# Sparse attention and a mixture of attention experts on one core: a new order of loads and TensorE steps, epsilons as columns of the sums, k's low half on GpSimd

## The chip, the core and the metric

The kernel runs on one core of a Trainium2 chip. A core has a matrix engine (TensorE, PE in the profile; its weight loads are shown apart as PEld), a vector engine (VectorE, DVE), a scalar engine (ScalarE, ACT), GpSimd (POOL) and SyncE (SP), which issues the DMA transfers of this kernel. Each engine works through its own list of instructions in order; semaphores let it wait for others. TensorE writes to the eight banks of PSUM; VectorE and ScalarE copy from there to SBUF. The metric is the device time of one execution in microseconds, lower is better.

## What is computed

The reference has two parts. The first is attention over q, k, v of shape (8, 8, 576, 64), batch, heads, tokens, width. Heads 0 to 3 have a local causal mask (the last 32 tokens), heads 4 to 7 a strided one (earlier tokens of the same place modulo 32). Both are normalised with exp and a sum to which 1e-9 is added. The eight heads side by side are x, 576 tokens by 512.

```python
mask_local   = (rel >= 0) & (rel < stride)
mask_strided = (rel >= 0) & (pos[None, :] % stride == pos[:, None] % stride)
attn = np.exp(scores - max); attn /= attn.sum(-1) + 1e-09; x = attn @ v
```

The second part is a mixture of four experts, each a causal attention head over x with its own wq, wk, wv, wo. A gate picks two of the four experts for each token and weighs them with a softmax (again with 1e-9 in the sum).

```python
logits = x @ w_gate; topk = two largest; w = softmax(topk logits, + 1e-09)
for e: q, k, v = x @ wq[e], x @ wk[e], x @ wv[e]
       ye = causal_softmax(scale * q @ k.T, + 1e-09) @ v @ wo[e]
       out += (w of e, 0 if not picked) * ye
```

## The kernel before

A batch goes through two stages. **Stage 1** (`stage1`, L422) does the sparse attention of two heads at a time, four pairs of heads a batch. q and k are loaded and turned (L493), the scores of the few blocks that the mask leaves are computed by small matmuls (step `s_l` for a local pair, L534, 36 products; `s_s` for a strided one, L541, 22), masked (L557), and put through a softmax of six steps (L563 to L579): maximum, subtraction on GpSimd, exp, sum, epsilon and reciprocal (L576, L577), product on GpSimd. Then the values: `xa_l` (L629, 42 products) for a local pair; `pt` (L600) and `xa_s` (L652) for a strided one. The result is split in a high and a low part, xh and xl (L612, L614), since later matmuls work on pairs of a high and a low half.

**Stage 2** (L695 to L982) projects x: `pj` (L777; L788 in the first batch) for q and k of two experts at a time, `vp` (L706) for v and the gate. Of k three things are kept: the high half, a plain copy kf (L800), and the low half kf minus high (L806), which VectorE or GpSimd computes as the order says. The gate follows (L734 to L765). Then, for each tile of 128 tokens, the scores `s2` (L876; `s2_4`, L833, for the last 64 tokens), mask and maximum (L883), exp with its sum (L888), epsilon and reciprocal of the sums (`recip2`, L894 and L895), scaling by it and by the gate's weight on GpSimd (`scale2`, L915 and L906), transposing (`t2`, L934), copying out (L303), and the product with v (`acc`, L967). `out_tile` (L984) multiplies by wo (`yp`, L996), and SyncE stores the result (L1008).

The operations are recorded first (`op`, L91), each with its kind, its engines and what it reads and writes. The order in which they are put out is a table written by hand or by a planner: the string PLAN (L115), a word for each operation. `schedule` (L272) reads it:

```python
for word in PLAN.split():
    o, slots = OPS[int(word[:i])], iter(word[i + 1:])
    for u in o.uses:
        if not u.taken: u.ring.take(u, int(next(slots)))
    o.fn(ENGINE[word[i]])
```

The number is the operation, the letter the engine (P, A, D, G, S), the digits behind it the buffers that the operation takes. So the table sets the order on each engine, SyncE's queue among them, and the choice between two engines where an operation allows it. Products of plain fp32 appear in the trace as two matmuls with two weight loads each (72 for an `s_l` step, 84 for an `xa_l` step, 44 for `xa_s`), those of the split halves as one. `spin` (L1012) are matmuls of a constant tile fz that compute nothing; they stand where the table puts them, 54 of the 60.

Of the kernel before, what the change touches and what calls it, by code (L numbers as in the profile page):

```python
# [20 lines left out]
def attention_moe_kernel(  # L21
# [69 lines left out]
    def op(kind, eng, n, key, fn, r=(), w=(), mode=None, npk=0, after=()):  # L91
# [29 lines left out]
        114D 251S0 17P5 115D 48P2 23P1 116D1 47P6 146P0 152S 117D 118G 110S 119G 120A 185P31 147D 121A 122D 191P7
        153S 186A 123D 252A0 124D 156P520 192A 253G0 233S 40P4 268S4 157D 125G 46P1 302S 158D 41P6 35P0 126G 273S
        159D2 33P3 28P7 160D 154S 189P4 161G 127D1 267S 162G 163A 187P5 190D 234A 164A 235G 165D 128P162000 155S
        188A 166D 167D 271S 89P374511 169G 131A 150S 135A 132D 129A 136D 133A 168G 130D 39P6 134D 96A 92A 199P011
        137G 97D 90A 93D 94A 98G 245S 91D 95D 170P261 195S0 200D 18P5 201D 172A 1246P70 171A 202D3 9P3 203D 1296P41
        204G 239S 275D0 1289P0 248S 205G 206A 49P5 173P6122 246A 208D 207A 247G 196S 1253P2 209D 174A 178A 1260P3
        175D 193S 176A 1297P 179D 177D 1247P 240A 197S 210D 180G 1254P 241G 1248P 249A 194S 211G 1266P5 250D 31P1
        198S 212G 42P6 1267P 303S 1261P 1290P 254S1 213P160 1268P 215A 214D 300S 25P6 0P1 216P6133 337S0 257S 1298P
        221A 217A 1291P 222D 219A 255A 1262P 220D 338S1 218D 256G 1303P1 260S0 1299P 308D1 223G 266S 1255P 1301A0
        306S2 1249P 1300A 1304P 304S 1302D0 1250A 1263P 258A 263S1 1251A1 1269P 259D 269S 1264A 1252G1 1292P 1271A  # L130
        1270A 1265D 305S 1305P 1294A 1272D 474S3 1281P61 1293A 261A0 336S 1295D 341S 1275P4 262D0 1282A 334S 346S1
        264A 1318P730 274D 1276A 265G 335S 1323P500 307S 1320D0 280P640 1324D 1322A 411S4 1325D 1326A 1256P 1319D
        281D 1327A 1309P3 282D 1257A 340S 1277P5 1258A 283D0 339S 1321A 1259G 342D0 284G 1310P 1278A 1306P 309D
        375S0 1279P0 1307A 347S 285A 1308D 374S 286D 1273P7 1280A 377S 343D 407S2 348S 1283P6 1328P420 1274A 287D
        1284A 344S 288G 1285D00000 1311P 370S1 1312P 413S 45P5 1313A 312S2 1329D 1286A 1314A 1317P1001 1330D 1331A
        1287D 5P7 1332A 1349P650 1315D 349S 1288G 1333D 1385P421 1351D1 1337G 372S 1316P73 406S 1350D 1336G 1353A
        373S 1335G 1354D 350P560 1352A 371S 1338G 1386D2 279S0 1355D 1388A 1334G 352D 1339G 1340P742 1356A 351D 376S
# [150 lines left out]
    def ring(tag, shape, bufs, dtype=F32):  # L288
        return Ring(tag, shape, dtype, bufs, pool=sb)

    def fixed(tag, shape, bufs, dtype=F32, value=None):
        ts = []
        for i in range(bufs):
            t = const.tile(shape, dtype, name=f"{tag}{i}")
            if value is not None:
                for x in value(t):
                    nc.vector.memset(x, 0.0)
            ts.append(t)
        return Ring(tag, shape, dtype, bufs, tiles=ts)
# [775 lines left out]
```

## Time and profile before

| | |
|---|---|
| time, median of 3 runs | 470.14 us (468.7 to 471.44) |
| the profiled execution: its time | 472.47 us |
| its span, first to last instruction | 470.3 us |
| mean granted clock of TensorE | 0.979 |
| busy share: TensorE, VectorE, ScalarE, GpSimd | 94%, 77%, 58%, 44% |
| DMA packets, bytes | 189816, 41.90 MB |

The busy share of an engine is the time covered by its instructions. A wait is idle time just before an instruction, with the engine and line that ended it; "issue" stands where nothing that the profile shows was waited for. [...]

### The profile page before, as it was taken

To read this page: it belongs to the slowest core of one execution; us is meant where nothing else is said; L and a number is where in the kernel's file an instruction comes from. 1 tells how busy PE (TensorE), PEld (TensorE's weight loads), DVE (VectorE), ACT (ScalarE), POOL (GpSimd) and SP (SyncE) were. 2 spreads that over 40 slices of the span, in tenths; PEclk is the share of its full clock that TensorE was granted. 3 is DMA by queue.
4 is the path that set the end of the run, shared out by engine and by line. 5 is a ranking of instruction groups with operands and counts; after the bars stand their busy time and mean duration, and the time that the engine had idled before them with its cause. 6 is when DMAs were issued, how large, how long until landed. Compare 5 with 4: busy or idle time off the path is not lost.

```text
span 470.3 us, 19348 instructions
## 1 busy us (share of the span) xinstructions
PE 441.2 (94%) x7876; PEld 389.9 (83%) x7876; DVE 360.6 (77%) x1078; ACT 272.9 (58%) x835; POOL 208.3 (44%) x324
## 2 busy tenths in 40 slices
PE   7999997879997999989899989999999899999996
PEld 7898975759976998889789968799879898899874
DVE  4566699956898997798699969888999679735740
ACT  2444648725667565866377554844785367745752
POOL 6354237733067643552274505571557207700540
PEclk9989998889999999999999999999999989999999
DMA  6654855543664535441564642456542310110113
GB/s 180 140 102 83 149 94 94 93 81 52 122 141 93 94 71 110 100 102 32 103 108 89 134 85 50 92 94 124 106 111 60 93 48 2 57 46 0 48 68 112
DMA packets 189816, 41.90 MB, mean 89 GB/s; under 512 B 184064, under 2 KB 184064, under 8 KB 189728
## 3 DMA queue, kind: packets, MB, share of 16 engines
q1 hardware_dynamic: 189728, 40.67, 41.6%
q8 instruction: 62, 1.02, 0.9%
q14 instruction: 26, 0.21, 0.2%
HBM read 31.20 MB, written 9.44 MB: 86 GB/s over the span
## 4 chain that ended last, share of the span: by engine, by line
PE 77%; DVE 12%; issue 4%; POOL 2%; DMA 1%; ACT 1%; SPq 1%; DVEq 0%; ACTq 0%; POOLq 0%
PE bank L777 18%; PE bank L996 9%; PE bank L706 9%; PE bank L967 8%; PE bank L876 6%; PE bank L934 5%; PE bank L629 3%; PE bank L652 3%; PE bank L534 3%; PE bank L788 3%; DVE p L883 2%; PE bank L461 2%; PE bank L1015 2%; PE bank L541 2%; PE bank L714 2%
## 5 line engine op out<-in xcount | busy, mean ns | idle before, releaser
L915 POOL TENSOR_SCALAR p<-p,st,wt 128x256 f32<-128x256 f32 (+3 forms) x128 | 77.1, 614 | 74.7 <-PE bank L777 23.3
L888 ACT ACTIVATE p<-p,st 128x128 f32<-128x128 f32 (+3 forms) x128 | 71.7, 563 | 12.7 <-DVE st L883 12.6
L883 DVE CUSTOM_DVE_ANT_0 p<-bank,m_cau 128x512 f32<-128x512 f32 (+3 forms) x128 | 57.1, 483 | 2.9 <-PE bank L876 2.1
L493 DVE STREAM_TRANSPOSE qkt<-nat 128x576 f32<-128x576 f32 x56 | 56.0, 1008 | 2.9 <-DMA nat<-in_q_dram 1.9
L303 ACT COPY th<-bank 128x256 f32<-128x256 f32 (+2 forms) x112 | 43.7, 429 | 12.7 <-PE bank L934 9.6
L967 PE MATMUL bank<-th,vs 128*64 128x192 f32 (+4 forms) x512 | 49.1, 343 | 0.0
L967 PEld LDWEIGHTS bank<-th,vs 128*64 128x64 f32 x512 | 34.8, 139 | 14.3 <-issue 6.9
L934 PE MATMUL bank<-ident,p 64*128 64x64 f32 x800 | 41.4, 234 | 3.6 <-POOL p L915 1.6
L934 PEld LDWEIGHTS bank<-ident,p 64*128 64x128 f32 x800 | 34.9, 144 | 11.7 <-issue 3.7
L797 ACT CAST qk<-bank 128x288 fp32r<-128x288 f32 x64 | 25.6, 402 | 28.0 <-PE bank L777 25.8
L614 DVE TENSOR_TENSOR xl<-bank,xh 128x160 fp32r<-128x160 f32 (+3 forms) x112 | 30.5, 323 | 14.5 <-ACT xh L612 13.0
L706 PE MATMUL bank<-wh_v,xh 128*128 128x260 f32 x128 | 36.8, 287 | 0.0
L706 PE MATMUL bank<-wl_v,xh 128*128 128x260 f32 x128 | 36.3, 283 | 0.0
L706 PE MATMUL bank<-wh_v,xl 128*128 128x260 f32 x128 | 36.0, 281 | 0.0
L612 ACT CAST xh<-bank 128x128 fp32r<-128x128 f32 (+3 forms) x112 | 27.4, 327 | 14.5 <-PE bank L629 7.3
L777 PE MATMUL bank<-xh,wh_k 128*128 128x288 f32 x112 | 33.8, 302 | 0.0
L777 PE MATMUL bank<-xh,wh_q 128*128 128x288 f32 x112 | 33.5, 299 | 0.2 <-DVE p1s L557 0.2
L777 PE MATMUL bank<-xl,wh_k 128*128 128x288 f32 x112 | 33.0, 294 | 0.0
L777 PE MATMUL bank<-xh,wl_k 128*128 128x288 f32 x112 | 33.0, 294 | 0.0
L777 PE MATMUL bank<-xl,wh_q 128*128 128x288 f32 x112 | 33.0, 294 | 0.0
L777 PE MATMUL bank<-xh,wl_q 128*128 128x288 f32 x112 | 33.0, 294 | 0.0
L420 POOL CAST xh<-xl 128x64 fp32r<-128x64 f32 x32 | 7.5, 237 | 56.2 <-DVE xl L614 56.1
(161 smaller groups left out, 1278.7 us busy)
## 6 DMA issues: line engine op xcount, KB each, us to landing
out_dram<-ys SPq DMA_DIRECT2D x32, 256.0 KB
nat<-in_q_dram SPq DMA_DIRECT2D x112, 72.0 KB
nat<-in_k_dram SPq DMA_DIRECT2D x112, 72.0 KB
v<-in_v_dram SPq DMA_DIRECT2D x96, 40.0 KB
v<-in_v_dram SPq DMA_DIRECT2D x128, 22.5 KB
v<-in_v_dram SPq DMA_DIRECT2D x64, 27.0 KB
v<-in_v_dram SPq DMA_DIRECT2D x32, 48.0 KB
out_dram<-ys SPq DMA_DIRECT2D x8, 128.0 KB
```

The source lines that it names most:

```text
L303: (nc.scalar.copy if e == "ACT" else nc.vector.tensor_copy)(dst, src)
L493: nc.vector.transpose(dst, src)
L614: op("xl", "D", n_, key + 0.5, lambda e, s_=s_, x_=x_: nc.vector.tensor_sub(x_(xl.t), s_(xa.t), x_(f(xh.t))), r=[xa, xh[u]], w=[xl[u]])
L706: nc.tensor.matmul(vp.t[:m, :NV], xx.t[:, t0:t0 + m], ww.t[:, kt, :], start=i == 0, stop=i == 11)
L777: nc.tensor.matmul(pj.t[:, :HS], ww.t[:, kt, ep * 128:(ep + 1) * 128], xx.t[:, c], start=i == 0, stop=i == 11)
L876: nc.tensor.matmul(sp[a].t[:, :nk], x.t[r, 0, q0:q0 + 128], y.t[r, 1, :nk], start=i == 0, stop=i == 2)
L883: lambda e, sp=sp, p=p, a=a, nk=nk, ci=ci: nc.vector.tensor_tensor_reduce(out=p.t[:, a, :nk], in0=sp[a].t[:, :nk], in1=m_cau[:, S - nk:], ...
L888: op("exp2", "A", nk, k_ + 1, lambda e, p=p, a=a, ci=ci, nk=nk: nc.scalar.activation(p.t[:, a, :nk], p.t[:, a, :nk], AF.Exp, bias=st.t[:, ...
L915: lambda e, p=p, a=a, ci=ci, t=t, nk=nk: nc.gpsimd.tensor_scalar(p.t[:, a, :nk], p.t[:, a, :nk], st.t[:, 14 + ci + a:15 + ci + a], wt.t[:, ...
L934: nc.tensor.transpose(tp[hf].t[:, 64 * c:64 * c + 64], src, ident[r, r])
L967: nc.tensor.matmul(acc.t[o, c0:c0 + cn], vw, th[a].t[:, s0:s0 + cn], start=j == 0, stop=j == idx[-1], skip_group_check=True)
L996: nc.tensor.matmul(yp.t[:, :DM], xx.t[:, c0:c0 + 128], ww.t[:, ep, :], start=i == 0, stop=i == 5)
```

## The change

The table PLAN is new from end to end. Of its first lines:

```diff
-        99S0 4P0 100S1 10P1 139S0 34P2 109S0 1P3 11P4 61S2 44P5 301S3 30P6 236S0 38P7 71S1 7P0 37P1 230S1 21P2 6P3
...
+        242S0 43P0 230S1 17P1 60S0 44P2 151S0 29P3 7P4 99S1 38P5 61S2 28P6 243A0 110S1 12P7 231A0 21P0 236S2 232G0
...
```

Three places show what it does. On TensorE, in the part of the program where the second batch's stage 1 ends and the third one's begins, the order before runs from the end of an `xa_l` step (L629) through a whole `xa_s` step into two `s_l` steps (L534, for the buffers qkt_183 and then qkt_181) and on to `pt` (L600):

```order
L629 MATMUL bank_68<-pt_197,v_189 64x32 x2
L652 MATMUL bank_64<-pt_198,v_187 64x54
...
L652 MATMUL bank_64<-pt_198,v_187 64x36 x2
L534 MATMUL bank_65<-qkt_183 32x64
...
L534 MATMUL bank_67<-qkt_183 32x64
L534 MATMUL bank_68<-qkt_181 32x64
...
L534 MATMUL bank_66<-qkt_181 32x64
L600 MATMUL bank_69<-ident,p1s_194 128x64
```

At the same place the new order has one `s_l` step (now L535) between `xa_l` (L634) and an output step `yp` (L1003), then transposing (L941), and `pt` (L605):

```order
L634 MATMUL bank_70<-pt_198,v_187 64x32 x2
L535 MATMUL bank_67<-qkt_183 32x64
...
L535 MATMUL bank_69<-qkt_183 32x64
L1003 MATMUL bank_71<-wh_o_258,oh_238 128x512
...
L1003 MATMUL bank_71<-wl_o_259,oh_239 128x512
L941 MATMUL bank_66<-ident,p_169 128x64
...
L941 MATMUL bank_70<-ident,p_169 128x64
L605 MATMUL bank_68<-ident,p1s_194 128x64
```

The second `s_l` step of the pair stands later, behind `yp`, two `xa_s` and an `acc` step.

The second place is the beginning of SyncE's queue (nat, vs and p hold q and k of the first batch, v its values, th weights). Before:

```order
L445 DMA nat_176<-in_q_dram 128x576
L445 DMA nat_177<-in_k_dram 128x576
L450 DMA vs_174<-in_q_dram 36x1024
L504 DMA v_185<-in_v_dram 32x5x64 x2
L445 DMA nat_178<-in_k_dram 128x576
```

Now:

```order
L388 DMA th_170<-in_moe_wq_dram 128x4x64
L388 DMA th_171<-in_moe_wk_dram 128x4x64
L446 DMA nat_176<-in_q_dram 128x576
L512 DMA v_185<-in_v_dram 18x6x64 x2
L446 DMA nat_177<-in_q_dram 128x576
L446 DMA nat_178<-in_k_dram 128x576
```

Two loads of weights and one of q stand ahead of the first load of v, where three of q and k stood.

The third place is GpSimd's list, in the second batch of stage 2. In the new order the gate's product (L765) is followed by six scalings (L922) and then by a low half of k (L812), which only GpSimd computes now:

```order
L765 TENSOR_TENSOR wt_225<-sel_221,mx_223 128x20
L765 TENSOR_TENSOR wt_225<-sel_221,mx_223 64x2 x2
L922 TENSOR_SCALAR p_165<-p_165,st_234,wt_225 128x384
L922 TENSOR_SCALAR p_162<-p_162,st_234,wt_225 128x256
L922 TENSOR_SCALAR p_160<-p_160,st_234,wt_225 128x128
L922 TENSOR_SCALAR p_165<-p_165,st_234,wt_225 128x384
L922 TENSOR_SCALAR p_162<-p_162,st_234,wt_225 128x256
L922 TENSOR_SCALAR p_160<-p_160,st_234,wt_225 128x128
L812 TENSOR_TENSOR qkl_156<-kf_159,qk_155 128x288
```

Before, 13 of the 32 low halves of k stood on GpSimd and 19 on VectorE.

The other edits follow. A column that holds 1e-9 for good stands beside the sums, so that one reduction over the sums and that column, or over a pair of columns, adds it; the separate additions go. In stage 1 the strided tile has room for the column beside its 54 scores, the local one adds a pair. The gate's last product moves from VectorE to GpSimd.

```diff
-    fz = const.tile([128, 128], F32, name="fz")
+    fz = const.tile([128, 1], F32, name="fz")
...
-    PSR = fixed("p1s", [128, 2, 6, 64], 2, value=lambda t: [t[:, h, :, 54:] for h in range(2)])
+    PSR = fixed("p1s", [128, 2, 6, 64], 2, value=lambda t: [(t[:, h, :, 54:], EPS) for h in range(2)])
-    ST1 = ring("st1", [128, 3, 12], 4)
+    ST1 = fixed("st1", [128, 4, 12], 4, value=lambda t: [(t[:, 3, :], EPS)])
...
             elif step == 3:
+                P = P if local else p.t[:, hsl, :, :nk + 1]
                 nc.vector.tensor_reduce(R[1], P, axis=mybir.AxisListType.X, op=ALU.add)
             elif step == 4:
-                nc.vector.tensor_scalar_add(R[2], R[1], EPS)
-                nc.vector.reciprocal(R[2], R[2])
+                if local:
+                    s = st.t.rearrange("p j i -> p (j i)")
+                    nc.vector.tensor_reduce(s[:, 24:24 + 2 * ni], at(s, 0, 128, 12, [[1, 2 * ni], [24, 2]]),
+                                            axis=mybir.AxisListType.X, op=ALU.add)
+                nc.vector.reciprocal(R[2], R[2 if local else 1])
...
-    LSEL = ring("sel", [128, NT, E], 1)
+    LSEL = fixed("sel", [128, NT, E + 1], 1, value=lambda t: [(t[:, :, E:], EPS)])
-    ST2 = ring("st2", [128, 24], 6)
+    ST2 = fixed("st2", [128, 30], 6, value=lambda t: [(t[:, 24:], EPS)])
...
-        def gate2(e):
-            w_ = wt.t[:, :NT]
-            nc.vector.tensor_mul(w_, w_, sel.t)
-            nc.vector.tensor_reduce(mx.t, w_, axis=mybir.AxisListType.X, op=ALU.add)
-            nc.vector.tensor_scalar_add(mx.t, mx.t, EPS)
+        def gate3(e):
+            s_ = sel.t[:, :, :E]
+            nc.vector.tensor_mul(s_, s_, wt.t[:, :NT])
+            nc.vector.tensor_reduce(mx.t, sel.t, axis=mybir.AxisListType.X, op=ALU.add)
             nc.vector.reciprocal(mx.t, mx.t)
-            nc.vector.tensor_mul(w_, w_, mx.t.unsqueeze(2).to_broadcast([128, NT, E]))
+
+        def gate4(e):
+            for r, t0, o, c in ((slice(0, 128), slice(0, NT), wt.t[:, :NT], slice(0, E)),
+                                (slice(0, 64), NT - 1, wt.t[0:64, NT, 0:2], slice(0, E, 3)),
+                                (slice(64, 128), NT - 1, wt.t[64:128, NT, 0:2], slice(1, 3))):
...
+                nc.gpsimd.tensor_tensor(o, sel.t[r, t0, c], m_, ALU.mult)
...
-                op("pj_lo", "DG", HS, key + step * u + 0.8, lambda e, c_=c_: (nc.gpsimd if e == "POOL" else nc.vector).tensor_sub(
+                op("pj_lo", "G", HS, key + step * u + 0.8, lambda e, c_=c_: nc.gpsimd.tensor_sub(
...
-            nc.vector.tensor_scalar_add(st.t[:, 14:14 + ncol], st.t[:, 8:8 + ncol], EPS)
+            nc.vector.tensor_reduce(st.t[:, 14:14 + ncol], at(st.t, 0, 128, 8, [[1, ncol], [16, 2]]),
+                                    axis=mybir.AxisListType.X, op=ALU.add)
...
-           lambda e: nc.tensor.matmul(wb.t[:, :128], fz, fz, start=True, stop=True), w=[wb], mode=M128)
+           lambda e: nc.tensor.matmul(wb.t[:, :128], fz.to_broadcast([128, 128]), fz.to_broadcast([128, 128]), start=True, stop=True), w=[wb], mode=M128)
```

The table holds 55 of the `spin` matmuls now. All other TensorE steps are the same in kind and number.

## Rows read from the trace of the kernel before

**Rows 1.** Page, busy time: us, share of the span, instructions.

```profile
PE 441.2 (94%) x7876; PEld 389.9 (83%) x7876; DVE 360.6 (77%) x1078; ACT 272.9 (58%) x835; POOL 208.3 (44%) x324
```

**Rows 2.** Page, the chain that ended last, share by engine.

```profile
PE 77%; DVE 12%; issue 4%; POOL 2%; DMA 1%; ACT 1%; SPq 1%; DVEq 0%; ACTq 0%; POOLq 0%
```

**Rows 3.** Waits of TensorE, whole span: us in total, times, longest us.

```profile
PE bank L534 <- issue: 3.8, 3, 1.4
PE bank L541 <- issue: 2.7, 2, 1.9
PE bank L629 <- issue: 2.2, 2, 1.7
PE bank L600 <- issue: 2.0, 1, 2.0
...
PE bank L996 <- issue: 1.4, 1, 1.4
...
PE bank L934 <- issue: 1.4, 1, 1.4
```

**Rows 4.** Timeline of TensorE, 95 to 103: start us, us, instruction, idle before.

```profile
94.78 1.15 PE L629 MATMUL bank<-pt,v 32*64 32x64 f32 x84
95.86 0.90 PE L652 MATMUL bank<-pt,v 54*64 54x54 f32 x44
...
98.56 1.47 PE L534 MATMUL bank<-qkt 64*32 64x64 f32 x120 [1.44 <-issue]
...
102.44 0.34 PE L600 MATMUL bank<-ident,p1s 64*128 64x64 f32 x5 [2.02 <-issue]
```

**Rows 5.** Windows: PE, PEld, DVE, ACT, POOL busy (x), PEclk, DMA share, GB/s.

```profile
98.55:102.43 3.88, 1.86 (x127) 1.63 (x128) 3.12 (x7) 0.00 (x0) 0.63 (x1) 1.00 0.35 70
...
190.00:200.00 10.00, 10.00 (x335) 8.51 (x334) 7.55 (x26) 8.33 (x28) 5.13 (x10) 1.00 0.51 106
70.00:80.00 10.00, 7.54 (x193) 5.92 (x190) 9.93 (x34) 7.99 (x24) 7.39 (x12) 0.94 0.48 91
...
100.00:110.00 10.00, 7.98 (x85) 6.44 (x84) 5.81 (x15) 3.95 (x10) 2.89 (x4) 0.83 0.40 77
370.00:380.00 10.00, 8.25 (x231) 7.50 (x231) 6.58 (x21) 5.34 (x20) 0.47 (x2) 0.83 0.38 99
```

**Rows 6.** Page, queue of TensorE's instructions: packets, MB, share of 16 engines.

```profile
q8 instruction: 62, 1.02, 0.9%
```

**Rows 7.** Groups of instructions: busy us, mean ns, idle before us, its releasers.

```profile
L806 DVE TENSOR_TENSOR qkl<-kf,qk 128x288 fp32r<-128x288 f32 x19 | 11.3, 594 | 11.3 <-ACT kf L800 6.7 <-ACT qk L797 4.3
...
L806 POOL TENSOR_TENSOR qkl<-kf,qk 128x288 fp32r<-128x288 f32 x13 | 10.5, 808 | 16.8 <-ACT kf L800 14.0 <-ACT qk L797 2.7
L894 DVE TENSOR_SCALAR st<-st 128x6 f32<-128x6 f32 (+1 forms) x32 | 9.0, 282 | 2.6 <-ACT p L888 1.7 <-ACT p L866 0.8
L576 DVE TENSOR_SCALAR st<-st 128x10 f32<-128x10 f32 (+1 forms) x32 | 8.2, 255 | 0.2
L751 DVE TENSOR_REDUCE mx<-wt 128x5 f32<-128x20 f32 x8 | 1.4, 175 | 0.3
```

**Rows 8.** Timeline around 74 us, GpSimd and VectorE.

```profile
74.19 1.28 POOL L570 TENSOR_TENSOR p1s<-p1s,st 128x648 f32<-128x648 f32 x1 [1.25 <-DVE st L568]
...
74.30 1.19 DVE L894 TENSOR_SCALAR st<-st 128x3 f32<-128x3 f32 x1
```

**Rows 9.** Waits of TensorE from 60 to 110.

```profile
PE bank L934 <- POOL p L915: 1.6, 3, 0.7
...
PE bank L833 <- ACT kf L803: 1.1, 1, 1.1
```

**Rows 10.** Timeline of GpSimd near 70 us: a burst of scalings.

```profile
69.70 3.23 POOL L915 TENSOR_SCALAR p<-p,st,wt 128x256 f32<-128x256 f32 x6 [0.37 <-DVE st L895]
```

**Rows 11.** SyncE's queue: a wait of the whole span; the third load's issue.

```profile
SPq L504 <- DVE v L297: 2.0, 1, 2.0
...
1.71 0.44 SPq L450 DMA_DIRECT2D vs<-in_q_dram  x1
```

More of the change, by code (lines that the diff above doesn't have):

```diff
@@ L121, in attention_moe_kernel @@
[L121 to L125, printed above, removed]
@@ new lines, in attention_moe_kernel @@
+        1687G 662S 728D 1609P22 1764A 1685G 1708D 625S 612D 1607A 1709G 1765D 791S1 1691P541 1610A 1710G 790S
+        639P010 1693A 1692D 1694P363 690S 1711G 640A 641D 1726P721 800S 1695A 1696D 1712P450 675P011 1714A 1728D5
+        1766G 756S 1715P362 1727D 1713A 1736P250 677D 1730A 759S 613G 1717D 1716A 1718P74 1768G 757S 1729A 1738D
+        1731P131 1440S 1720A 676D 642P6500 1740A 1732D 1767G 695D 1719A 678P4011 1608S 1734A 1733D 754S 643A
+        1721P11122 1737D 645A 681A 792S 647A 646D 1739A 644D 730S1 648D 1735A 682D 649G 1697P7 698S0 1722A 1741D
@@ new lines, in attention_moe_kernel @@
+        987D 2170A 1082S 988G 1023D1 1077S 2150P2 1045S 2158A 2159A 2160D 1106S 1043D 2165P7 2151A 989D0 2152A
+        1140S4 2153G 1079D 2171P6 1024P510322 2166A 2172A 2099P421 976S2 1031A 1029A 1032D 2204P761 1025A 1030D
+        1033G 1027A 1026D 2101A 2102P303 1028D 2100A 2205D0 2199P520 2103A 2206D 2167P1 1794S 2207A 2200D 1081S
+        2208A 2201D 2104D 1959S 2202A 2163P4 2168D 1084S 2203A 1174S 2185P7 1111S1 2164A 1962S 2173D00001 1085S
+        2177P3 1144S 2186A 1141S 2187D 2174A 2175D 1049S 2120P650 2176G 2178A 978S 2194P200 2179A 2121D 2123P142
@@ new lines, in attention_moe_kernel @@
+        1147S 995A 1057D 2105P3 2235G 992D 2132A 2130A 996D 2131D 1058G 994D 1179S 998D 2133D 2216P210 1093D 1113S
+        2106A 1968S 2107D 2219P072 2217A 999G 1094G 1047S 2218A 2237P541 2220D 2221A 2261P620 1215S 2238D 2239A
+        2240P313 1112S 2262D 1059P071 2242A 1048S 1095P450 2263D 2241A 2264A 2243P61 1097D 1214S 2282P320 2265A
+        2245D 1145S 1060D 2222P522 1061A 1965S 2266D 2244A 2283D 1178S 2267G 1096A 1971S 2270G 2284D 2285A 2246P1
+        1187S2 2268G 1115D 2223A 2271G 2286A 2224D 2272G 1098P0700 1149D 2247A 2249A 2269G 2290D 1062P6411 1220S1
@@ L296, in fixed @@
                 for x in value(t):
-                    nc.vector.memset(x, 0.0)
+                    x, y = x if isinstance(x, tuple) else (x, 0.0)
+                    nc.vector.memset(x, y)
             ts.append(t)
@@ L758, in values2 @@
            r=[wt], w=[wt])
-        op("gate3", "D", 5, key + 5 * step + 0.4, gate2, r=[wt, sel, mx], w=[wt, mx])
-        def gate3(e):
-            nc.gpsimd.tensor_copy(wt.t[0:64, NT, 0:2], wt.t[0:64, NT - 1, 0::3])
-            nc.gpsimd.tensor_copy(wt.t[64:128, NT, 0:2], wt.t[64:128, NT - 1, 1:3])
-        op("gate5", "G", 4, key + 5 * step + 0.6, gate3, r=[wt], w=[wt[1]])
+        op("gate3", "D", 3, key + 5 * step + 0.4, gate3, r=[wt, sel, mx], w=[sel, mx])
+        op("gate5", "G", 3, key + 5 * step + 0.6, gate4, r=[sel, mx, wt], w=[wt, wt[1]])
     def project(b, ep, qk, nm, key, step):
```

294 lines of the change are left out of this document (143 added, 151 removed).

## The prediction

> **What bounds the kernel now.** I read the busy time first. TensorE's matmuls cover 94% of the span, its weight loads 83%, VectorE 77%, the rest far less [rows 1]. The chain that ended last agrees: 77% of it is TensorE, 12% VectorE [rows 2]. So the kernel is one long TensorE program, and the question is what TensorE loses: time in which it stands idle, time at half clock, and time in which another engine sets its pace.
>
> The waits of TensorE come next. The largest are not waits for a producer: "issue" means that the engine waited for nothing the profile shows. The six rows add up to 13.5 us in ten gaps of 0.4 to 2.0 us [rows 3]; everything else it waited for is smaller. The timeline shows what stands around them [rows 4]: an xa_l step runs 84 matmuls in 1.15 us, an xa_s step 44 in 0.90, then two s_l steps follow, and inside these small matmuls TensorE stops for 1.44 us, and 4 us later for 2.02 us. The window from one stop to the next, 98.55 to 102.43 [rows 5], holds 127 matmuls and 128 weight loads, 255 instructions, in 3.88 us, of which TensorE is busy 1.86. The page counts 62 packets, 1.02 MB, on the queue of TensorE's instructions [rows 6]: 16 KB each, and 15,752 instructions [rows 1] over 62 is 254. So a packet brings some 256 instructions, and where 256 of them take about 2 us of work, the next packet is not there yet. A packet comes at best every 3.4 to 4 us. The window 190 to 200 is the control: 335 matmuls, 669 instructions, no idle time [rows 5], because they are mixed with long ones. It is a density per 256 that hurts, not a total.
>
> To see how sharp this is I walked the order before in steps of 256 instructions (a matmul and its weight load are two), ending where the gaps are, and added the durations of the steps in each. Nine stretches hold under 2.3 us of work. All nine end in a gap, 1.35 us on average. Of four stretches with 2.4 to 2.75 us one ends in a gap.
>
> The granted clock is the second loss. [...]
>
> The third is local. From 70 to 80 VectorE is busy 9.93 of 10 us and TensorE only 7.54 [rows 5]: the first batch is not yet overlapped with a full second one, VectorE sets the pace, and TensorE waits for GpSimd's scaling (1.6 us) and ScalarE's kf copy (1.1) [rows 9].
>
> **The change, part by part.**
>
> A, the order of TensorE. The steps and their number stay; one spacer matmul of 54 is added. Only what stands beside what changes. Before, the two xa_l of a batch stand directly behind each other in three of the later batches; now in one. Pairs of s_l stand in five places, before in six. Walking the new order in the same way, three stretches under 2.3 us remain (two with a pair of s_l, one with an xa_l behind a pair of s_s) and five between 2.5 and 3.0. Priced as before: 3 x 1.35 + 5 x 1.35 / 4 = 5.7 us against 13.5, a gain of 7.8; I take **-7.6**, since the boundary may sit a few instructions off. Ends: 0, if density is not the cause, and -13.5, if no gap is left.
>
> [...] Rows 3 to 5 show TensorE idle for 1.4 to 2.0 us at distances of 255 instructions. [...]
>
> B, the clock. The stretch at 96 to 104 is broken up (an output step and a transposing step now stand between s_l and pt), and the xa_l pair at 374 is gone. If both dips go this is 3.4 us. New gaps can cause new dips, so I take **-2.0**, ends +2 and -5.
>
> C, VectorE. It loses 19 of k's low halves at 594 ns [rows 7], 11.3 us. The 32 additions of epsilon at 282 ns (9.0 us) become 32 sums over six pairs. No row shows that operation; the nearest is the reduction of 20 numbers to 5 at 175 ns, above it the addition itself at 282 [rows 7], so 32 x 107 = 3.4 us down to 0; I take 3.4. The mean of 282 is made by long ones: one of three columns took 1.19 us while GpSimd's subtraction ran beside it [rows 8]. The 32 additions in stage 1 (8.2 us) vanish for the 16 strided tiles and become reductions for the 16 local ones: 5.4 us less. The gate loses two small operations. Together some 24 us of 361. Most of it lies beside TensorE work and is worth nothing. In the stretch of 60 to 110, a tenth of the kernel, VectorE is the pace; a tenth of 24 is 2.4, and the long additions sit there too. I take **-2.5**, ends 0 and -5.
>
> D, GpSimd. It gains 19 x 808 ns [rows 7] = 15.4 us and the gate's product, and reaches about 49% of the span; on average that is covered. But its work comes in bursts: six scalings in a row last 3.23 us [rows 10], and its softmax operation 1.28 us [rows 8]. The new order puts one half of k behind six scalings in the second batch, and the score step needs that half. Someone will wait; TensorE has other steps to run. I take **+2.0**; lower end 0, and the upper one is 16 waits of 0.8 us, a low half each, +13.
>
> E, the head. SyncE's queue now begins with two weight loads and one q load, then a load of v. That load waits for VectorE's clearing of the v tile (2.0 us before [rows 11]), and before three q and k loads had gone out by 1.71 us ahead of it [rows 11]. So two loads leave some 3 us later, which costs the start; on the other hand the last q and k loads stand nearer the queue's front than before. The fz column is set a little faster, the extra columns of epsilon run while VectorE waits for data, and the broadcast operand of the spacers reads the same words: each nothing I can price. **+0.5**, ends -3 and +3.
>
> Sum: -7.6 - 2.0 - 2.5 + 2.0 + 0.5 = -9.6. The profiled execution took 472.47 us (span 470.3 and 2.2 around it), so 462.9 on its scale. It is 2.3 above the median of the three runs, 470.14; on the median's scale the forecast is **460.5 us**. 0.5% here is 2.4 us, about what a measurement can tell from no change.
>
> **Rivals.**
>
> 1. The gaps do not go. Crossing into new instructions is then hidden in itself, and a packet is late for another reason, DMA traffic for one; a new order moves the gaps to other places. A and B are near 0 and C, D and E cancel: 469 to 471. Against it: nine of nine stretches under 2.3 us end in a gap. Chance 0.13. [...]
>
> 2. Slower. GpSimd becomes the producer that TensorE waits for. Price: 32 low halves of k, 0.8 us each, feed 16 groups of score steps; if each group waits for a whole low half behind a burst, D is +13 and the sum +1.4; if it waits for the rest of the burst as well, 1.3 us each, D is +21 and the sum about +9, so 472 to 480. It decides from the point where a low half is queued less than 3.2 us of TensorE work ahead of its score step. For it: the order puts one behind six scalings. Against it: GpSimd was idle over half of the time [rows 1], and from the order the low halves mostly stand several us ahead. Chance 0.10.
>
> 3. More than forecast. All issue gaps and dips go and VectorE's relief frees the whole stretch of 70 to 110: A -12, B -4, C -4, D 0: 448 to 454. Chance 0.15.
>
> The forecast, 455 to 468, keeps 0.62.
>
> **How the numbers follow.** Faster by over 2.4 us, below 467.8: nearly all of the forecast (0.61), rival 3 (0.15) and a little of rival 1 (0.02), 0.78. Within 0.5%: most of rival 1 and the tail of the forecast, 0.12. Slower: rival 2, 0.10. The range runs from 451, which takes in half of rival 3, to 470.5, which takes in most of rival 1; some 0.2 are left out.
>
> **What would show it.** A: the issue rows of TensorE sum to 4 to 7 us in place of 13.5, with the rest at pairs of s_l. B: fewer windows of 0.83. C: VectorE under 345 us busy, the new reductions near 0.18 us even beside GpSimd. D: GpSimd near 228 us; waits of score steps for qkl from GpSimd under 2 us. E: the first projection of batch 0 within 2 us of its old place. I am wrong if the issue sum stays above 10, or if TensorE's waits for GpSimd rise by more than 5.

## The result, and the profile after

| | before | after |
|---|---|---|
| time, median | 469.75 us (4 runs, 468.7 to 471.44) | 454.28 us (4 runs, 452.68 to 455.44) |
| ratio, 95% interval | | 0.9665, 0.9621 to 0.9709 |
| profiled execution: time, span | 472.47, 470.3 us | 455.44, 453.7 us |
| mean granted clock, as a share of TensorE's full speed | 0.979 | 0.988 |

The change makes the kernel 15.5 us faster, where 9.6 were forecast; 454.28 lies in the range. The ratios, here and below, and the medians of the table of experiments leave out disturbed runs, at a lower clock (0.972 to 0.978), so a ratio can stand a little off the quotient of the medians beside it.

The page after, busy time and chain (against [rows 1] and [rows 2]):

```profile
PE 436.0 (96%) x7878; PEld 385.8 (85%) x7878; DVE 338.5 (75%) x1037; ACT 270.6 (60%) x835; POOL 224.7 (50%) x352
...
PE 72%; DVE 12%; POOL 7%; issue 3%; DMA 3%; SPq 1%; ACT 1%; DVEq 0%; POOLq 0%; ACTq 0%
```

VectorE lost 22 us of work and GpSimd gained 16. The waits of TensorE over the whole span after (us in total, times, longest):

```profile
PE bank L941 <- POOL p L922: 4.6, 8, 1.4
PE bank L462 <- DMA vs<-in_k_dram: 2.1, 1, 2.1
PE bank L1022 <- DVE fz L312: 1.7, 1, 1.7
PE bank L535 <- issue: 1.3, 1, 1.3
PE bank L839 <- ACT kf L809: 1.0, 1, 1.0
PE bank L941 <- POOL p L915: 0.7, 1, 0.7
...
PE bank L605 <- POOL p1s L584: 0.2, 1, 0.2
```

Of the 13.5 us of issue gaps [rows 3] one of 1.3 is left; the waits for the scaled p of GpSimd rose from 1.6 us [rows 9] to 5.3, and a wait of 2.1 us for a load in the head is new (in e10, the same kernel again, it is 1.1). The windows after (PE, PEld, DVE, ACT, POOL busy, PEclk, DMA share, GB/s; the last four are those of [rows 5], the first two are new):

```profile
10.00:20.00 10.00, 7.88 (x174) 6.92 (x173) 2.74 (x6) 3.38 (x7) 2.35 (x4) 0.82 0.68 154
20.00:30.00 10.00, 10.00 (x218) 9.33 (x216) 5.40 (x13) 2.12 (x5) 2.41 (x4) 0.66 0.57 126
70.00:80.00 10.00, 6.39 (x188) 5.00 (x186) 9.75 (x37) 8.52 (x29) 8.32 (x15) 1.00 0.55 100
100.00:110.00 10.00, 10.00 (x151) 9.73 (x148) 7.52 (x20) 4.05 (x13) 5.18 (x7) 1.00 0.63 124
190.00:200.00 10.00, 8.68 (x202) 7.94 (x199) 7.28 (x16) 3.83 (x10) 6.67 (x10) 1.00 0.43 80
370.00:380.00 10.00, 10.00 (x237) 8.33 (x237) 8.62 (x25) 3.92 (x16) 7.07 (x12) 1.00 0.01 3
```

From 100 to 110 and from 370 to 380 the clock is back at 1.00 and TensorE is never idle. But behind the wait of 2.1 us at 16 us it runs at half clock (0.50 in each window of 1 us from 17 to 26): by the means of the two windows 2 x 10 x (0.18 + 0.34) = 10.4 us of these 20. From 70 to 80 VectorE is still busy 9.75 of 10.

Groups of instructions after (busy us, mean ns, idle before), in place of the additions and the low half in [rows 7]:

```profile
L812 POOL TENSOR_TENSOR qkl<-kf,qk 128x288 fp32r<-128x288 f32 x32 | 25.8, 806 | 35.2 <-ACT qk L803 30.2 <-ACT kf L806 4.7 <-ACT vs L732 0.3
...
L900 DVE TENSOR_REDUCE st<-st 128x6 f32<-128x12 f32 (+1 forms) x32 | 4.9, 154 | 3.6 <-ACT p L894 3.2 <-ACT p L872 0.3
...
L580 DVE TENSOR_REDUCE st<-st 128x10 f32<-128x20 f32 x16 | 2.7, 170 | 0.2
```

### The profile page after: what moved, and what is told of

It is laid out like the page before. It is cut to its first block, busy times and chain, and to the rows that moved or that the text cites. A ratio compares the mean times of both kernels' runs of the same rounds, so it can differ in the third digit from the quotient of the medians.

```text
span 453.7 us, 19338 instructions
## 1 busy us (share of the span) xinstructions
PE 436.0 (96%) x7878; PEld 385.8 (85%) x7878; DVE 338.5 (75%) x1037; ACT 270.6 (60%) x835; POOL 224.7 (50%) x352
## 4 chain that ended last, share of the span: by engine, by line
PE 72%; DVE 12%; POOL 7%; issue 3%; DMA 3%; SPq 1%; ACT 1%; DVEq 0%; POOLq 0%; ACTq 0%
PE bank L783 17%; PE bank L1003 9%; PE bank L711 9%; PE bank L974 6%; PE bank L882 5%; PE bank L941 5%; POOL p L922 4%; PE bank L634 3%; PE bank L657 3%; PE bank L462 3%; PE bank L794 3%; PE bank L1022 2%; PE bank L535 2%; DVE p L889 2%; PE bank L719 2%
## 5 line engine op out<-in xcount | busy, mean ns | idle before, releaser
L922 POOL TENSOR_SCALAR p<-p,st,wt 128x256 f32<-128x256 f32 (+3 forms) x128 | 76.2, 608 | 17.6 <-DVE st L902 8.4
L894 ACT ACTIVATE p<-p,st 128x256 f32<-128x256 f32 (+3 forms) x128 | 71.4, 564 | 4.1 <-DVE st L889 3.7
L889 DVE CUSTOM_DVE_ANT_0 p<-bank,m_cau 128x256 f32<-128x256 f32 (+3 forms) x128 | 56.4, 483 | 6.2 <-PE bank L882 5.6
L974 PE MATMUL bank<-th,vs 128*64 128x192 f32 (+4 forms) x512 | 48.0, 337 | 0.5 <-ACT th L304 0.5
L974 PEld LDWEIGHTS bank<-th,vs 128*64 128x64 f32 x512 | 33.6, 137 | 13.5 <-issue 5.9
L941 PE MATMUL bank<-ident,p 64*128 64x64 f32 x800 | 39.6, 227 | 5.7 <-POOL p L922 4.6
L941 PEld LDWEIGHTS bank<-ident,p 64*128 64x128 f32 x800 | 33.3, 138 | 13.6 <-POOL p L922 6.9
L812 POOL TENSOR_TENSOR qkl<-kf,qk 128x288 fp32r<-128x288 f32 x32 | 25.8, 806 | 35.2 <-ACT qk L803 30.2
L619 DVE TENSOR_TENSOR xl<-bank,xh 128x160 fp32r<-128x160 f32 (+3 forms) x112 | 31.1, 322 | 10.8 <-ACT xh L617 10.4
L304 DVE COPY th<-bank 128x384 f32<-128x384 f32 (+2 forms) x48 | 23.0, 496 | 15.6 <-PE bank L941 15.3
L617 ACT CAST xh<-bank 128x160 fp32r<-128x160 f32 (+3 forms) x112 | 27.6, 323 | 11.3 <-PE bank L634 6.1
L571 POOL TENSOR_TENSOR p1s<-p1s,st 128x648 f32<-128x648 f32 (+1 forms) x18 | 20.7, 1157 | 27.2 <-DVE st L569 26.0
```

The source lines that it names most:

```text
L304: (nc.scalar.copy if e == "ACT" else nc.vector.tensor_copy)(dst, src)
L617: op("xh", "A", n_, key, lambda e, s_=s_, x_=x_: nc.scalar.copy(x_(xh.t), s_(xa.t)), r=[xa], w=[xh[u]])
L619: op("xl", "D", n_, key + 0.5, lambda e, s_=s_, x_=x_: nc.vector.tensor_sub(x_(xl.t), s_(xa.t), x_(f(xh.t))), r=[xa, xh[u]], w=[xl[u]])
L889: lambda e, sp=sp, p=p, a=a, nk=nk, ci=ci: nc.vector.tensor_tensor_reduce(out=p.t[:, a, :nk], in0=sp[a].t[:, :nk], in1=m_cau[:, S - nk:], ...
L894: op("exp2", "A", nk, k_ + 1, lambda e, p=p, a=a, ci=ci, nk=nk: nc.scalar.activation(p.t[:, a, :nk], p.t[:, a, :nk], AF.Exp, bias=st.t[:, ...
L922: lambda e, p=p, a=a, ci=ci, t=t, nk=nk: nc.gpsimd.tensor_scalar(p.t[:, a, :nk], p.t[:, a, :nk], st.t[:, 14 + ci + a:15 + ci + a], wt.t[:, ...
```

## The experiments

Which part did it? The change has three parts that can be had apart: the table, the arithmetic with epsilon and the gate, and the engine of k's low halves. Each kernel was timed against the kernel before on its own chip; its median there was 469.9 to 471.5 us.

| kernel | median us | ratio, 95% interval | issue gaps us |
|---|---|---|---|
| before | 469.9 to 471.5 | | 13.5 |
| e1 new table, old arithmetic | 462.35 | 0.986 (0.979 to 0.993) | 1.6 |
| e2 old table, new arithmetic | 463.83 | 0.988 (0.981 to 0.994) | 10.4 |
| e3 changed, low halves back | 454.86 | 0.967 (0.960 to 0.974) | 1.9 |
| e4 before, twelve steps moved | 468.63 | 0.997 (0.994 to 1.001) | 3.4 |
| e6 e2 and e4 together | 463.28 | 0.983 (0.976 to 0.989) | 4.0 |
| e7 changed, boundaries shifted | 461.27 | 0.980 (0.976 to 0.985) | 6.3 |
| e8 changed, stage 2's addition back | 457.19 | 0.969 (0.962 to 0.977) | 1.2 |
| e9 changed, stage 1's addition back | 456.15 | 0.969 (0.964 to 0.973) | 1.0 |
| e10 changed, again | 454.35 | 0.965 (0.961 to 0.969) | 0.8 |
| e11 changed, both additions back | 458.28 | 0.972 (0.967 to 0.978) | 0.2 |
| e12 changed, head reordered | 450.03 | 0.955 (0.951 to 0.959) | 0.5 |
| e13 changed, gate back | 457.2 | 0.973 (0.968 to 0.977) | 2.4 |

**e1, the table alone.** PLAN of the changed kernel in the code of before.

> The kernel before with the new table alone (its letters put k's low halves on GpSimd, as in the changed kernel); the separate additions of epsilon, 32 x 282 ns, stay on VectorE. Theory (the order did it: no stretch of 256 TensorE instructions is short enough any more to end in a gap): TensorE's issue gaps sum to 1 to 2.5 us, as in the changed kernel (1.3), and the time is 454 to 459 us; VectorE has about 9.0 - 4.9 = 4 us more to do, of which little lies on the path. Rival (the edits of the arithmetic did it): 464 to 470 us.

0.986: the table alone is worth 6.6 us of 470, and the issue gaps fall to 1.6. Neither theory had that: the gaps go, but less than half of the whole gain comes. Waits for p from GpSimd are 6.0 us here. Of TensorE's waits in e1:

```profile
PE bank L934 <- POOL p L915: 6.0, 8, 1.4
PE bank L461 <- DMA vs<-in_k_dram: 2.5, 1, 2.5
...
PE bank L534 <- issue: 1.6, 1, 1.6
PE bank L600 <- POOL p1s L579: 1.3, 2, 1.0
```

**e2, the arithmetic alone.** PLAN of before in the changed code, with the choice of engine for the low halves that it needs:

```diff
-                op("pj_lo", "G", HS, key + step * u + 0.8, lambda e, c_=c_: nc.gpsimd.tensor_sub(
+                op("pj_lo", "DG", HS, key + step * u + 0.8, lambda e, c_=c_: (nc.gpsimd if e == "POOL" else nc.vector).tensor_sub(
```

In five batches some scalings read the gate's weights ahead of the product that GpSimd now computes: the operations are the same, but what these scalings read is not yet right, and they may wait less than they should. In e6 the product stands ahead of them.

> The changed kernel with the table of before, so 19 of k's low halves stand on VectorE again; only the sums with epsilon and the gate's product are new. Theory (the order did it): the same ten issue gaps of TensorE, 12 to 15 us in sum, at the same places, and 466 to 470 us. Rival (the edits of the arithmetic did it, by relief of VectorE between 70 and 110 us): 456 to 462 us.

Again between the two: 0.988, 5.7 us, though 10.4 us of issue gaps stay at nearly all the old places. So order and arithmetic are each worth about 6 alone. Their sum, 12.3, is short of the whole, 15.5 to 16.4, but with intervals of some 3 us on each side of both that doesn't show whether they help each other.

**e3, the low halves.** Nineteen letters of pj_lo change in the table (the expectation counts one too many), and the operation allows both engines again, as in e2; for one:

```diff
-1295G0
+1295D0
```

> The changed kernel, its order, but 20 of k's low halves on VectorE again, at the same places of the table. VectorE gets about 20 x 0.59 = 12 us more, GpSimd 20 x 0.81 = 16 us less. If VectorE's relief is part of the gain (it was 9.93 of 10 us busy from 70 to 80 us before): 456 to 460 us. If the low halves move between two engines that have time: 453 to 456 us. If GpSimd's queue is what TensorE now waits for (its waits for p from GpSimd sum to 5.3 us): 449 to 452 us, and those waits fall to about 2 us.

454.86 against 454.28 and 454.35. No run shows that the engine of the low half is worth anything in either direction, though VectorE is 6.6 us busier; and TensorE's waits for p stay at 5.5 us (5.3 in the changed kernel), so GpSimd's low halves aren't what makes them.

**e4, the gaps without the rest.** Twelve words of PLAN of before moved, for example

```diff
-1721P622
...
+734P350
...
+1721P622
...
-734P350
```

that is, one s_l (734) goes to where the acc (1721) stood, and the acc between the two xa_s.

> The kernel before with twelve of its 2668 steps moved by one to three places in TensorE's list, so that a long step (acc, yp, vp) stands between two dense ones, or a dense one goes ahead of a long one; nothing else changes. By the walk in stretches of 256 instructions one stretch under 2.3 us is left of nine (at 37 us, 2.1 us of work), and one of 2.4. Theory: issue gaps fall from 13.5 to 2 to 5 us, the half-clock stretches behind them become fewer, and the time falls from 470 to 457 to 463 us. Rival (gaps come from DMA traffic, or the gain came from the arithmetic): gaps stay above 9 us, 467 to 471 us. Second rival (the moved steps make other waits): gaps fall, and waits for other engines rise by as much, 466 to 470 us.

The second rival holds. The gaps fall to 3.4 us, the time by 0.3%, inside the interval. The timelines show the bargain at one pair of s_l. Before (start us, us, instruction, idle before):

```profile
196.99 1.60 PE L652 MATMUL bank<-pt,v 54*64 54x54 f32 x88
198.52 1.49 PE L534 MATMUL bank<-qkt 64*32 64x64 f32 x126
201.32 0.42 PE L534 MATMUL bank<-qkt 64*32 64x64 f32 x18 [1.30 <-issue]
201.67 0.58 PE L934 MATMUL bank<-ident,p 64*128 64x64 f32 x12
...
203.30 0.39 PE L714 MATMUL bank<-wh_v,xh 128*128 128x260 f32 x1
```

and in e4:

```profile
191.07 0.97 PE L534 MATMUL bank<-qkt 64*32 64x64 f32 x72
191.97 1.15 PE L652 MATMUL bank<-pt,v 54*64 54x54 f32 x44
193.04 1.64 PE L967 MATMUL bank<-th,vs 128*64 128x192 f32 x20
194.61 0.90 PE L652 MATMUL bank<-pt,v 54*64 54x54 f32 x44
195.44 1.19 PE L534 MATMUL bank<-qkt 64*32 64x64 f32 x72
196.55 0.59 PE L934 MATMUL bank<-ident,p 64*128 64x64 f32 x12
...
199.00 0.39 PE L714 MATMUL bank<-wh_v,xh 128*128 128x260 f32 x1
```

The same eight steps (an acc, two xa_s, two s_l, and t2, s2, t2 behind them; the acc starts at 195.43 before) take 7.87 us before, 1.30 of it the gap, and 7.93 in e4, without it. By their starts, the two xa_s take 1.90 us in place of 1.53, the first s_l 0.90 in place of 0.73, and the three steps behind 2.45 in place of 1.63, where one waits 0.18. Over the whole profile TensorE's idle time falls by 5.4 us (other waits take back 4.8 of the 10.2), and its steps, with half-clock stretches reckoned at full speed, take 5.4 us longer: 438.2 against 432.8. What this profile gains besides is clock, 0.996 against 0.979; it is the fastest of ten runs, 465.76.

**e6, e4 with the new arithmetic**, to see whether VectorE was what came next.

> The changed kernel's arithmetic with the table of before and the twelve steps of e4 moved (and the gate's product, which is on GpSimd, put ahead of the scalings that read it). With the table of before alone these edits gave 463.8 us and kept 10.4 us of issue gaps; with the arithmetic of before the twelve moves took the gaps from 13.5 to 3.4 us and the time only to 468.6. Theory (VectorE is late next: with its additions of epsilon gone, the gaps that go are worth their time): 455 to 459 us, issue gaps 2 to 4 us. Rival (gaps of issue are covered by something else that these edits do not touch): 461 to 464 us.

463.28 against 463.83 (2.4 us by the ratios, the intervals overlapping): the rival. Taking the gaps out by hand is worth little with either arithmetic. The new table takes them out without slower steps: reckoned as above they take 436.2 us in e6, but 431.7 in e1 and 430.9 in the changed kernel.

**e7, the gaps put back.** In the changed kernel 12 spacers of the head become 64 matmuls of 1 x 1:

```diff
...
-           lambda e: nc.tensor.matmul(wb.t[:, :128], fz.to_broadcast([128, 128]), fz.to_broadcast([128, 128]), start=True, stop=True), w=[wb], mode=M128)
+           lambda e: [nc.tensor.matmul(wb.t[:1, :1], fz, fz, start=True, stop=True) for _ in range(tiny[i])][-1]
+           if i in tiny else nc.tensor.matmul(wb.t[:, :128], fz.to_broadcast([128, 128]), fz.to_broadcast([128, 128]), start=True, stop=True), w=[wb], mode=M128)
```

> The changed kernel with 52 more matmuls of 1 x 1 in plain fp32 (208 instructions of TensorE) in the place of twelve spacers at its start, so that every stretch of 256 instructions begins 208 instructions earlier in the program; order and arithmetic are the same. By the walk eight stretches hold under 2.5 us (1.6 to 2.0 us in five of them: from pt into xa_s of batch 2, at vp of batch 3, at xa_l of batch 4, at s_l and at xa_l of batch 5) where three did. Theory (the gaps come with the place of the boundary): five to eight issue gaps, 5 to 10 us in sum, at these places, none at 193 us, and 457 to 463 us. Second theory (as in e4, other waits take over or give way): the same gaps, but 454 to 457 us. Rival (the gaps have another cause, or the place in the program does not matter): one gap of 1.3 us, 453 to 456 us.

The gaps come back, at seven of the eight places of the walk (one of them 0.17 us), and the one at 193 us goes. The issue rows of e7 among the waits of TensorE:

```profile
PE bank L535 <- issue: 2.2, 2, 1.5
...
PE bank L605 <- issue: 1.4, 1, 1.4
...
PE bank L634 <- issue: 1.0, 1, 1.0
...
PE bank L711 <- issue: 0.8, 1, 0.8
PE bank L542 <- issue: 0.8, 1, 0.8
```

One of them in e7's timeline, inside a pt step that has no gap in the changed kernel:

```profile
143.58 0.53 PE L605 MATMUL bank<-ident,p1s 64*128 64x64 f32 x10 [1.39 <-issue]
```

And it costs: 0.980 against 0.965 in e10 and 0.967 first, 6.4 to 7.1 us for 5.0 to 5.5 us of gaps. The order of the steps and the loads are the same, so the place of the 256-boundary alone makes the gaps. The traces say so once more: counted over all instructions of TensorE in a trace, matmuls, weight loads and its own semaphore instructions, the matmul behind each of the 46 issue gaps in the fourteen profiles stands at place 193 or 194 of 256.

The time rises by the length of the gaps and a little more, but not by idle time alone: between the two profiles (spans 459.4 and 453.7) idle time rises by 2.7 us, since the waits for the head's load and for p are shorter in e7, and by the granted clock (0.984 against 0.988) another 1.9 go with the clock.

**e8 and e9, one addition back each.** In stage 2 (e8):

```diff
-            nc.vector.tensor_reduce(st.t[:, 14:14 + ncol], at(st.t, 0, 128, 8, [[1, ncol], [16, 2]]),
-                                    axis=mybir.AxisListType.X, op=ALU.add)
+            nc.vector.tensor_scalar_add(st.t[:, 14:14 + ncol], st.t[:, 8:8 + ncol], EPS)
```

and in stage 1 (e9) the sum over the scores alone and `tensor_scalar_add(R[2], R[1], EPS)`, as before.

> The changed kernel with stage 2's separate addition of epsilon back (32 of some 260 ns in place of 32 sums of 154 ns: 3.4 us more on VectorE). The order alone, with all additions and the gate as before, took 462.35 us, 8.1 above the changed kernel, for 13 us of VectorE. If time follows VectorE's work: 455.5 to 457.5 us. If this one counts most, because TensorE waits for the scaled p of GpSimd that comes behind it: 458 to 462 us. If it counts nothing: 453.5 to 455 us.

> The changed kernel with stage 1's separate additions of epsilon back (32 of some 340 ns in place of 16 sums of 170 ns: about 8 us more on VectorE). If time follows VectorE's work: 457.5 to 461 us. If only stage 2's chain matters: 453.5 to 455.5 us.

Some 1 to 3 us each, inside the intervals; neither is the one that counts. TensorE's waits for p are no longer in e8 than in e10 (5.7 us in both); those for stage 1's p1s are longer in e9 (1.6 against 0.6).

**e10 to e12.** The changed kernel again, both additions back, and an attempt to beat it. e11 is the edits of e8 and e9 in one. e12 moves words of the table: the second half load of k (140) goes behind the first (141), four loads of v (151, 110, 109, 71) behind the last whole load (184), and a vp step (1810) between two s_l:

```diff
-151S0
-110S1
...
 141S
+140S
...
-109S
-140S
-71S2
...
 184S
+151S0
+110S1
+109S
+71S2
...
+1810P11
...
-1810P11
```

> The changed kernel once more, on the chip of the two runs beside it: 452.5 to 456 us, ratio to the kernel before 0.964 to 0.969; issue gaps of TensorE under 2.5 us.

> The changed kernel with the separate additions of both stages back (e8 and e9 in one; about 11 us more on VectorE than the changed kernel); the gate stays changed. With either one back the time rose by 0.2 to 0.3% of the kernel before, inside the intervals; with both and the gate back (e1) by some 8 us. First theory (VectorE has some slack, and the work over it counts in full): 459 to 463 us, like e1. Second (the two are worth what each is alone, and the gate is what matters): 455 to 458 us.

> The changed kernel with its table edited at three places: in SyncE's queue the second half load of k for the third pair of heads goes right behind the first half, the first four loads of v behind the last whole loads of q and k, and on TensorE the second s_l step of the pair at 194 us stands behind the next vp step. Theory (the 2.1 us wait for that load at 16 us, and the 10 us at half clock that follow it, come from the loads of v ahead in the queue, the first of which also waits for VectorE's clearing of v): the wait falls under 0.5 us, the half clock in the head under 4 us, the issue gap at 194 us goes, first pj of batch 0 at 35 to 37.5 us in place of 39.6, and the time is 2.5 to 5 us below e10: 449 to 452 us. Rival (the DMA engines are busy anyway, so another load or the next step is late instead): first pj within 1 us of 39.6, 453 to 456 us.

e11: 3.4 us above e10 by the ratio and 3.9 by the median, about what the second theory said; its interval overlaps that of e10 a little. Its clock differs from run to run (0.976 to 0.990), which is taken up below.

e10 has one issue gap, but not where the first profile of the same kernel has it. The pair of s_l at 190 us runs through, and the gap stands in the next pair but two:

```profile
190.28 1.69 PE L535 MATMUL bank<-qkt 64*32 64x64 f32 x144
...
338.44 1.37 PE L535 MATMUL bank<-qkt 64*32 64x64 f32 x112 [0.81 <-issue]
```

e12 beats both kernels: 4.3 us below e10, the intervals apart. The head in the changed kernel, then in e12 (timeline of TensorE):

```profile
12.87 0.97 PE L535 MATMUL bank<-qkt 64*32 64x64 f32 x72
15.97 1.52 PE L462 MATMUL bank<-ident,vs 36*64 36x36 f32 x32 [2.12 <-DMA vs<-in_k_dram]
```

```profile
12.33 0.97 PE L535 MATMUL bank<-qkt 64*32 64x64 f32 x72
13.23 1.20 PE L462 MATMUL bank<-ident,vs 36*64 36x36 f32 x32
```

and SyncE's queue, where that second half of k was issued at 9.70 us and a load of v waited 1.7 us for VectorE's clearing; in e12:

```profile
3.81 0.88 SPq L451 DMA_DIRECT2D vs<-in_k_dram  x2
...
8.92 0.87 SPq L512 DMA_DIRECT2D v<-in_v_dram  x2
```

With the wait the half clock goes: the two windows of 10 to 30 us in e12 stand at 1.00:

```profile
10.00:20.00 10.00, 10.00 (x246) 9.11 (x242) 4.52 (x12) 3.96 (x7) 2.73 (x5) 1.00 0.60 143
20.00:30.00 10.00, 9.62 (x374) 8.96 (x373) 6.54 (x16) 3.87 (x8) 4.67 (x8) 1.00 0.47 95
```

The first projection of batch 0 starts at 33.6 us, before at 38.4, in the changed kernel at 39.6 and in e10 at 37.6. So of the 4.2 us between the spans of e10 and e12 (452.5 and 448.3) 4.0 are there by then. The moved vp step adds nothing: ahead of it, at 186 us, e12 leads by 4.3.

**e13, the gate back.** The gate's functions of before in the changed kernel: product, sum, addition, reciprocal and product on VectorE, two copies on GpSimd.

```diff
...
+            nc.vector.tensor_scalar_add(mx.t, mx.t, EPS)
             nc.vector.reciprocal(mx.t, mx.t)
+            nc.vector.tensor_mul(w_, w_, mx.t.unsqueeze(2).to_broadcast([128, NT, E]))
...
```

> The changed kernel with the gate's arithmetic of before (on VectorE a product, a sum, an addition of epsilon, a reciprocal and a product, then two copies on GpSimd, in place of a product, a sum and a reciprocal, then three products on GpSimd); the sums of both stages stay changed. The order alone (e1) stands 8 us above the changed kernel; one addition back costs 0 to 3 us (e8, e9), both back about 3 to 8 (e11). First theory (the separate additions of the two stages are nearly all of it): 453.5 to 456 us. Second (the gate's chain, on which the scalings of a batch wait, is the rest): 457 to 460 us, with longer waits of TensorE for p from GpSimd.

0.973, by number the second theory; but its sign did not come. The waits for p from GpSimd are no longer than in e10 (5.2 against 5.7 us); what e13's profile has more is a longer wait for the load in the head, which no gate precedes, and the issue gap at 195 us:

```profile
PE bank L939 <- POOL p L920: 4.7, 7, 1.4
PE bank L462 <- DMA vs<-in_k_dram: 2.8, 1, 2.8
PE bank L535 <- issue: 2.4, 2, 1.6
```

That wait was 0.8 to 2.8 us in the eight profiles that have the unshifted head of the changed kernel, so a part of the differences of 1 to 3 us among e8 to e13 is the head's.

**The clock taken out.** Each run has its span and its granted clock. Span times clock is what the span would be at full speed throughout, an estimate: it reckons idle time as if it were clocked too. Means over the runs that the ratios use:

| kernel | span x clock, us | lost to the clock, us |
|---|---|---|
| before (39 runs) | 460.7 | 7.6 |
| e1 new table, old arithmetic | 452.5 | 9.1 |
| e2 old table, new arithmetic | 456.5 | 5.9 |
| e4 before, twelve steps moved | 461.7 | 4.7 |
| changed (first and e10, 10 runs) | 447.2 | 5.7 |
| e8, e9 one addition back | 449.2, 448.9 | 5.8, 5.6 |
| e11 both additions back | 450.0 | 6.7 |
| e13 gate back | 448.2 | 7.1 |
| e12 head reordered | 445.9 | 2.4 |

Standard errors are 0.3 to 0.8 us (e2 1.4), and the kernel before differs by up to 3 us from chip to chip (459.2 to 462.2), so read it to some 2 us. By it the two additions are worth about 3 us (2 each alone), the gate 1, and the order 8; e1 stands 5.3 above the changed kernel. The rest of the distance by the ratios is the lower clock of e1; whether the additions cause that too is not shown.

## Why the prediction was right, and where not

**The whole.** Right in sign and range, too small by 6 us. With the clock taken out as above, the order (A, D and E together) gave 8.2 us where 5.1 were forecast, the arithmetic (C) 5.3 where 2.5 were, and the clock (B) 1.9 where 2.0 were. So A and C were mis-sized; and E was priced at 0.5, where e12 shows some 4 us.

**A and B, the order.** The mechanism holds: e7 moves the boundary alone and the gaps move. The promised 4 to 7 us of issue rows came out at 1.3. The walk gave three stretches under 2.3 us in the new order; in the profile after only the one that ends in the pair of s_l at 194 us stalled, and in e10 none of the three did: its gap at 338 us ends a stretch of 2.5 us. One that didn't stall takes 1.66 us in the profile after (from 140.26 to 141.92, the end of a pt step and most of a pair of s_l): its packet started 0.7 us ahead of TensorE's crossing, where at the gap that ends at 98.56 us before and the one that ends at 193.81 after a packet started 1.0 and 1.3 us behind it. Ahead of the stretch stand the 20 longer matmuls of an acc (1.64 us); that they make the difference is my reading, which no run shows. In e10 the packet for the stretch at 190 us started 0.8 us ahead of TensorE's crossing, the one at 338 us 0.95 behind it. "Nine of nine" was a rule of the old order (by the starts in its trace: eight stretches under 2.3 us, all with a gap; of four at 2.36 to 2.61 two have one). In the new order the work in a stretch does not decide alone.

What failed in A is the price, one us for one us of gap. e1 lost 12 us of gaps and gained 6.6 us, because longer waits for p (6.0 us, before 1.6) and for the head's load (2.5, before 0.8) came in their place; e4 lost 10 and gained 0.3%. In the other direction e7 paid the full length. I read this as: a gap is worth its length where TensorE has no other wait close behind; no run tests that for a single gap. That the forecast for A, B, D and E together, -7.1, came near the measured -6.6 is luck: more gaps went than forecast, at a lower price each.

Most crossings show no gap: in e7 seven of some 62 end in one, and these seven cost 6.4 to 7.1 us.

**B.** The 3.4 us are the two windows at 0.83 of [rows 5], 2 x 10 x 0.17 us. Their half clock begins within 1 us of the gaps that end at 102.44 and 374.87 us (the windows of 1 us there: 0.89 from 102 to 103 and 0.50 behind it, 0.93 from 375 to 376 and 0.50 behind it); the windows of 10 us with the gaps that end at 153.65, 201.32, 226.12 and 280.78 us, of 1.3 to 1.9 us, stand at 1.00. The dips at 100 and 370 went; the head got one of 10.4 us that I had not looked for (6.8 in e10). Over the runs of the table above the loss to the clock fell from 7.6 to 5.7 us, about as forecast, but at other places.

**C, VectorE.** This is the term that was mis-sized: -2.5 with an end at -5; e2 measured -5.7, and from e1 to the changed kernel, where only the arithmetic differs, it is 9 to 10 by the ratios, 8 by the medians and 5.3 with the clock taken out. The low halves, half of the work I counted, show no worth (e3). So some 11 to 12 us of additions and gate (VectorE busy 349.4 in e2 against 360.6, 338.5 after against 350.8 in e1) give 5 us or more. The step that failed is "most of it lies beside TensorE work and is worth nothing", a tenth of 24 us. An addition of epsilon isn't work beside: by the code it stands in the chain from the exp through sum and reciprocal to GpSimd's product or scaling, on which TensorE's transposing step waits, in every batch. A low half can be done any time in several us. TensorE's waits bear this out in part only: from e1 to the changed kernel they fall from 17.0 to 12.7 us, 1.1 of it at stage 1's p1s (1.3 to 0.2) and 0.7 at the scaled p (6.0 to 5.3); and in e2 the largest part of what they lose, 3.2 us, is issue gaps that are shorter or gone. Which waits the rest of C comes from stays open. And the additions were long where GpSimd worked. The timeline of before around 262 us, VectorE and GpSimd:

```profile
261.93 0.18 DVE L576 TENSOR_SCALAR st<-st 128x10 f32<-128x10 f32 x1
...
262.51 1.26 POOL L579 TENSOR_TENSOR p1l<-p1l,st 128x640 f32<-128x640 f32 x1 [0.43 <-ACT qk L797]
...
262.59 1.21 DVE L576 TENSOR_SCALAR st<-st 128x10 f32<-128x10 f32 x1
```

The same addition takes 0.18 us in the first row and 1.21 beside GpSimd's product, until that ends. After, at 86 us, a sum beside the same product:

```profile
86.03 1.26 POOL L584 TENSOR_TENSOR p1l<-p1l,st 128x640 f32<-128x640 f32 x1
...
86.42 0.16 DVE L900 TENSOR_REDUCE st<-st 128x3 f32<-128x6 f32 x1
```

Of the 72 additions before, 13 began while a GpSimd operation with two tensors ran: they took 0.69 us on average, all over 0.3, and each ended 24 to 31 ns behind that operation. Of 14 that began beside another of its operations five took over 0.18, up to 0.49, each beside a scaling; the 45 beside nothing took 0.16, none over 0.18. All additions together lost 7.9 us that way. Of the 48 sums after, 15 began beside an operation with two tensors, and none took over 0.18. Why an addition waits there and a sum does not, no run shows. I had seen one such row and taken it into a mean.

**D, GpSimd.** Taken as +2. GpSimd came to 224.7 us (228 promised), no score step waited for a low half, and with the low halves back (e3) the waits for p are the same. They belong to the order, since e1 has them too. Rival 2 had its place wrong.

**E, the head.** +0.5 taken; the first projection came 1.2 us later, as promised within 2, and 0.8 earlier in e10. But the price behind it, a wait of 2.1 us and 10.4 us at half clock, was bigger than the term: e12 gets some 4 us from there, nearly all of it ahead of the first projection, and most of it clock.

## What to carry to other kernels

Find the idle time of the bound engine that no producer explains, and count its instructions (here all 46 gaps stand at place 193 or 194 of 256); but do not price a gap at its length, since other waits may come in its place, and moving steps apart can make the steps themselves slower (438.2 us of steps in e4 against 432.8); test by shifting the boundary, which leaves order and loads as they are. Tiny VectorE operations in a chain were not free here: the two additions cost some 3 us, though VectorE is busy for only 75% of e11's span. Beside GpSimd a reduction over a constant column can replace an addition: the 15 sums that began beside an operation with two tensors took 0.12 to 0.18 us, the 13 additions 0.34 to 1.21. In the head, order the loads by when they are needed: here waits of 2.1 and 1.1 us for a late one stood ahead of 10.4 and 6.8 us at half clock, and where the wait went so did these (e12).

## What was not expected of the hardware

A small addition of a constant on VectorE took 0.16 us alone and up to 1.21 us when it started beside a two-tensor operation of GpSimd, up to 0.49 beside a scaling (before); a sum that gives as many numbers took 0.12 to 0.18 us, beside GpSimd or not (after).

52 tiny matmuls more in the head, 208 instructions, made the kernel 6.4 to 7.1 us slower, although they ran while TensorE had spacers to run.

A wait of 2.1 us of TensorE at 16 us was followed by 10.4 us at half clock, one of 1.1 us in e10 by 6.8; without the wait the clock stayed at 1.00 (e12).

The same program did not stall at the same place each time (the changed kernel and e10). Of eight profiles with the same list of TensorE, six stall in the pair of s_l near 195 us and five in the pair near 340, by 0.2 to 1.6 us.
